# Attention read followed by a soft mixture of experts: the dispatch division behind layer one, wider transfers, a new order

## The chip, the cores and the metric

The kernel runs on one core of a Trainium2 chip. The metric is the time on the device in microseconds (us), the median of three runs. Engines are written as in the profile: PE is the matrix engine, PEld its weight loads, DVE the vector engine, ACT the scalar engine, POOL the third elementwise engine, SP the engine whose queue issues nearly all DMA transfers.

## The reference, cut to what matters

All data are float32. The attention part makes 4,352 rows of 512 numbers; the expert part treats all of them as one batch.

```
# attention: x (8,8,512,64), state (8,8,32,64)
a     = softmax(x state^T / 8);  xread = a state
a2    = softmax(state x^T / 8);  sread = a2 x
rows  = concat(xread, sread)              # 4352 x 512 after regrouping
# soft mixture of experts: 8 experts, 4 slots each
logits = rows phi                         # 4352 x 32
d = exp(logits - max over rows); d /= sum over rows + 1e-9
slot_input = d^T rows                     # 32 x 512
h = relu(slot_input[e] w1[e]); slot_out[e] = h w2[e]
c = softmax(logits over the 32 slots)
out = c slot_out                          # 4352 x 512
```

The sum under d is positive, so relu(v / s) = relu(v) / s: the division may stand before or behind the first layer.

## The kernel before, in words

The 51 MB that move are x (8 batches), the two weight matrices (33.5 MB together) and the output (8.9 MB). Every instruction is placed by hand: `ORDER` is a list of steps such as `x1.7.0`, each name a small function, and every engine runs its own instructions in the order in which they come up there. A `!` behind a step sends its copy to DVE, otherwise to ACT. The lists `HOMES` say which buffer each new tile takes: `b` the eight PSUM banks, `h` eleven half tiles of 128x512, `big` five tiles of 8 KB a partition, `wide` eight of 16 KB a partition.

**The attention stage** (up to about 76 us) walks through the eight batches. For each batch and each half h of its heads: `X`, `xe` transpose and scale x; `S` makes the scores; `q`, `m1`, `sub`, `x1`, `l1`, `rr`, `mul`, `aT` are one softmax (DVE transposes and reduces, POOL subtracts and multiplies, ACT takes the exponential); `m2`, `e2`, `E`, `ee`, `R`, `sr` are the other; `A`, `ae` turn the first one's result back; `Lx` makes the logits of the batch. Batches go in pairs k = 0 to 3 into a running maximum, a running sum `l_row` and a running dispatch product `y`: `mx`, `mk`, `bm`, `nme` give the new maximum, `al` the factor by which what is there shrinks, `dx`, `dT`, `dTe`, `T`, `tt`, `Px` the pair's own product, and `Y` adds it as y = y * factor + part. The state rows do the same in two halves (`Ls`, `Lr`, `msx`, `als`, `dsx`, `D`, `Ps`, `Ys`). The last two additions are `Y.3` and `Ys.1`. Then `Wd`, `We` make the reciprocal `rl` of the sum, `SI` transposes y, and `SIe` multiplies by `rl` and spreads the result into `si_m`, a block-sparse operand zeroed ahead of time (`windows`).

**The first layer** is the steps `W`, 16 of them, eight matmuls each on the page's count, at line 805. `hc`, `ht`, `hr` copy, transpose, sum and rectify one half of the hidden units and spread it into `h_m`, zeroed by `hz` on POOL. **The second layer** is the steps `u.k.hf.e` at line 868, for four column blocks k of the output. Each block ends in `c.k` (copy), `s.k` (a matmul that sums the partial rows, and a copy of its result to `so_r`), `o.k.0` and `o.k.1` (four matmuls each with the combine weights, `os` for the state rows) and eight copies `oc.k.q.j` into the output tile. In between, `cm`, `cx`, `cd`, `cb` make the combine weights. One output transfer goes for each (k, q), two for those in `HALVED`.

**The loads** stand in `loads()`. Seven weight transfers are issued at the start; `ld.0` to `ld.15` are the rest. SP takes its transfers strictly in order, and each waits until its target buffer has been read for the last time: a `big` tile until the batch of x or the weight tile in it is used up, `w_half` until four half tiles are free, `w_an` until the two `an` tiles are.

Of the kernel before, what the change touches and what calls it, by code (L numbers as in the profile page):

```python
# [980 lines left out]
```

## Time and profile before

| what | value |
|---|---|
| median of 3 runs | 129.79 us (129.78 to 129.86) |
| the profiled execution, own time | 130.58 us |
| its span, first to last instruction | 128.8 us |
| PE, DVE, ACT, POOL busy | 115.7, 88.6, 74.1, 44.7 us |
| moved by DMA | 51.76 MB, 402 GB/s over the span |

The profiled execution is 0.79 us above the median, and 1.78 us of it lie outside its span. Busy time of PE counts pipelined matmuls from issue to a modelled end, so 90% busy does not mean PE at its peak. The DMA share is the mean over sixteen DMA engines and passes 1.00 in some stretches.

### The profile page before, as it was taken

Reading aid. Unit: us, or ns where it says so; the run is one execution under the profiler, and the core shown is the slowest. Engines: PE = TensorE matmul, PEld = TensorE weight load, DVE = VectorE, ACT = ScalarE, POOL = GpSimd, SP = SyncE. Lnnn points to the kernel's source line nnn. Section 1 sums busy time; section 2 is a strip of 40 time slices with the busy share of each in tenths; the row PEclk is TensorE's granted clock in tenths of the full one; section 3 lists DMA queues with packets and bytes.
Section 4 is the critical chain, followed back from the end, with each engine's and each line's share of the span. In section 5 each row is a group of like instructions: output and inputs, shape, how many; then the busy total and the mean of one; then the engine's idle time right before and its main releaser. Section 6 shows DMA issues by size and latency. Waiting matters only on the chain.

```text
span 128.8 us, 4863 instructions
## 1 busy us (share of the span) xinstructions
PE 115.7 (90%) x2080; PEld 83.6 (65%) x2080; DVE 88.6 (69%) x206; ACT 74.1 (58%) x178; POOL 44.7 (35%) x62
## 2 busy tenths in 40 slices
PE   6979999999999999999998969999999999998400
PEld 3647768588659769587887759934594667576100
DVE  3069999999999999999998687651073254173700
ACT  3038999999998899999953601030203753151600
POOL 2105175395459363386693205653010000000000
PEclk9999999999999999999999999999999999999955
DMA  4999999999999999999999999999999999999991
GB/s 90 374 401 453 417 438 399 445 417 455 415 407 458 427 412 417 416 421 425 438 445 417 415 408 410 420 425 433 435 443 407 389 396 416 417 384 420 374 416 78
DMA packets 7366, 51.76 MB, mean 402 GB/s; under 512 B 816, under 2 KB 944, under 8 KB 3760
## 3 DMA queue, kind: packets, MB, share of 16 engines
q1 hardware_dynamic: 7200, 51.19, 95.6%
q8 instruction: 16, 0.26, 0.7%
q10 hardware_dynamic: 144, 0.26, 0.6%
q14 instruction: 6, 0.05, 0.1%
HBM read 42.53 MB, written 8.91 MB: 399 GB/s over the span
## 4 chain that ended last, share of the span: by engine, by line
PE 54%; DVE 17%; ACT 16%; issue 5%; POOL 2%; DVEq 1%; POOLq 0%
PE so_ps L868 12%; PE h_ps L805 11%; PE o L897 7%; ACT xt L271 4%; PE spin L292 3%; ACT q L365 3%; DVE nm L437 3%; PE sc L340 3%; DVE q L353 3%; ACT e L442 2%; DVE m L358 2%; ACT eT L268 2%; DVE aT L384 2%; PE an_ps L450 2%; ACT an L268 2%
## 5 line engine op out<-in xcount | busy, mean ns | idle before, releaser
L271 ACT ACTIVATE xt<-xt_ps 128x512 f32<-128x512 f32 x30 | 16.9, 628 | 6.6 <-PE xt_ps L391 4.7
L362 POOL TENSOR_TENSOR q<-q,m 128x512 f32<-128x512 f32 x14 | 14.7, 1049 | 15.7 <-DVE m L358 9.2
L379 POOL TENSOR_TENSOR q<-q,rr 128x512 f32<-128x512 f32 x16 | 16.6, 1049 | 6.6 <-DVE rr L375 2.9
L326 PE MATMUL xt_ps<-ident,x 128*128 128x128 f32 x112 | 15.7, 277 | 0.0
L868 PEld LDWEIGHTS so_ps<-w,h_m 128*32 128x32 f32 x432 | 11.5, 110 | 6.1 <-issue 5.6
L868 PE MATMUL so_ps<-w,h_m 128*32 128x128 f32 x432 | 15.1, 275 | 0.0
L805 PE MATMUL h_ps<-w,si_m 128*32 128x512 f32 x128 | 14.6, 594 | 0.4 <-DVE si_m L776 0.4
L268 ACT COPY out<-o 128x512 f32<-128x512 f32 x18 | 9.5, 596 | 7.4 <-PE o L897 7.4
L326 PEld LDWEIGHTS xt_ps<-ident,x 128*128 128x128 f32 x112 | 12.4, 141 | 1.9 <-DVE q L353 0.8
L268 DVE COPY out<-o 128x512 f32<-128x512 f32 x14 | 9.1, 686 | 4.7 <-PE o L897 4.5
L442 ACT ACTIVATE e<-sc,nm 128x512 f32<-128x512 f32 x16 | 11.5, 724 | 0.0
L805 PEld LDWEIGHTS h_ps<-w,si_m 128*32 128x32 f32 x128 | 8.6, 110 | 4.1 <-issue 3.2
L384 DVE STREAM_TRANSPOSE aT<-q 128x512 f32<-128x512 f32 x16 | 10.9, 687 | 0.1
L365 ACT ACTIVATE q<-q 128x512 f32<-128x512 f32 x16 | 10.2, 655 | 1.1 <-POOL q L362 1.1
L437 DVE TENSOR_REDUCE nm<-sc 128x1 f32<-128x512 f32 x16 | 10.5, 662 | 0.0
L897 PE MATMUL o<-lt_all,so_r 32*128 32x512 f32 x64 | 10.3, 629 | 0.0
L368 DVE TENSOR_REDUCE ls<-q 128x16 f32<-128x512 f32 x16 | 10.2, 666 | 0.0
L353 DVE STREAM_TRANSPOSE q<-sc 128x512 f32<-128x512 f32 x14 | 9.8, 697 | 0.1
L450 PE MATMUL eT_ps<-ident,e 128*128 128x128 f32 x64 | 9.7, 280 | 0.0
L450 PE MATMUL an_ps<-ident,aT 128*128 128x128 f32 x64 | 9.5, 277 | 0.0
L268 ACT COPY eT<-eT_ps 128x512 f32<-128x512 f32 x16 | 9.3, 604 | 0.2
L358 DVE TENSOR_REDUCE m<-q 128x16 f32<-128x512 f32 x14 | 9.2, 661 | 0.1
(144 smaller groups left out, 198.4 us busy)
## 6 DMA issues: line engine op xcount, KB each, us to landing
w<-w_in SPq DMA_DIRECT2D x10, 2048.0 KB, 26.1
w<-w_in SPq DMA_DIRECT2D x9, 1024.0 KB, 13.6
out_x<-out SPq DMA_DIRECT2D x5, 1024.0 KB, 6.8
x<-x_in SPq DMA_DIRECT2D x2, 2048.0 KB, 15.5
out_x<-out SPq DMA_DIRECT2D x6, 512.0 KB, 5.5
x<-x_in SPq DMA_DIRECT2D x2, 1024.0 KB, 14.6
x<-x_in SPq DMA_DIRECT2D x2, 512.0 KB, 6.6
w_half<-w_in SPq DMA_DIRECT2D x4, 256.0 KB, 15.2
```

The source lines that it names most:

```text
L268: (dve.tensor_copy if Z["dve"] else act.copy)(out, in_)
L271: (dve.tensor_scalar_mul if Z["dve"] else act.mul)(out, in_, by)
L326: pe.transpose(p[:, P * j : P * j + P], x_at(b, g, j), ident)
L362: pool.tensor_tensor(v, v, R[b][f"m1{h}"].broadcast_to([P, 16, NS]), op=ALU.subtract)
L365: act.activation(R[b][f"q{h}"], R[b][f"q{h}"], AF.Exp)
L379: pool.tensor_tensor(v, v, R[b]["rr"][:, 16 * h : 16 * h + 16].broadcast_to([P, 16, NS]), op=ALU.mult)
L437: dve.tensor_reduce(out=r[f"nm2{h}"], in_=r[f"sp{h}"], axis=AX.X, op=ALU.max, negate=True)
L442: act.activation(r[f"e2{h}"], r[f"sp{h}"], AF.Exp, bias=r[f"nm2{h}"], accum_out=ls[:, b % 2, 32 + h, 0:1])
L450: pe.transpose(p[:, j, :], r[f"{src}{h}"][:, P * j : P * j + P], ident)
L805: pe.matmul(h_ps[hf][32 * kt : 32 * kt + 32, :], si_m[kt // 2][:, 256 * (kt % 2) + 32 * e : 256 * (kt % 2) + 32 * e + 32], wt[1, hf, e, kt ...
L868: pe.matmul(so[k][32 * i : 32 * i + 32, :], h_m[hf][:, 256 * i + 32 * e : 256 * i + 32 * e + 32], wt[2, c, e, 4 * hf + i][:, col : col + n ...
L897: pe.matmul(o[j], so_r[hf][rows, col : col + 128], lt_all[rows, 4 * q : 4 * q + 4, :].rearrange("p b s -> p (b s)"), start=True, stop=True,)
```

## The change

1. `SIe` becomes two plain copies, one for each tile of `si_m`, with no factor. `We` makes `rl` as before; `hr` now uses it: one instruction rectifies and multiplies all four blocks, one copy spreads them (before: four rectifying instructions that also spread).
2. The last two additions to y change places: `Ys.1` first, with a factor that carries y past both maxima at once (`al.3`), then `Y.3` adds the pair's product times the factor of the state half. `l_row` likewise.
3. The five `big` tiles and the eleven half tiles are slices of one tile each, so that a transfer can fill neighbours: the weight loads go out as 13 transfers behind the first seven instead of 20 in 16 steps, `w_half` as one of 1 MB instead of four, `w_an` as one instead of two, and six of the 1 MB loads as three of 2 MB. Block 1 of the output goes out as one transfer of 2 MB when all its eight copies are done (`WHOLE`), instead of two of 1 MB.
4. `ORDER` is new, and with it `HOMES`. The steps are the same but for `SIe` and `ld`.

```diff
 ORDER = """
...
-Y.1 Ve.1! Lr.1 ld.5 Lu.2 al.3 msx.1 als.1 Px.2 Ys.0 dsx.1 D.1 T.3 Ps.1 tt.3 Lu.3 Y.2 ld.6 ld.7 Px.3 Lus.1 Wd Y.3
-Ys.1 SI We SIe W.0.0 cm.0 W.0.1 W.0.2 W.0.5 ld.8 ld.9 ld.10 W.0.6 W.0.7 W.0.3 ld.11 cx.0 W.0.4 hc.0 W.1.0 lkp.1!
...
+nme.2 ee.7.0 srT.4 l1.6.1 rr.6 V.0 ae.5.0 sr.5 ld.2 x1.7.1
+l1.7.1 R.6.0 R.6.1 srT.5 sub.7.0 mul.6.0 ae.5.1 srTe.4 R.7.0 x1.7.0 l1.7.0 ee.7.1 R.7.1 sr.6 dx.2 srTe.5 rr.7 aT.6.0
...
+ld.3 Ls.1 Px.1 A.6.1 nme.3 dx.3 dT.3 Lse.1 Lr.1 tt.2 al.2 keep.3 Y.1 Ps.0 dTe.3 ae.6.1! T.3 Lus.0 msx.1 Ve.1! Ue.1
+dsx.1 Px.2 D.1 Ps.1 Lu.2 Ys.0 ld.4 al.3 Lus.1 lkp.1 als.1 tt.3 ld.5 ld.6 Px.3 Y.2 Ys.1 Y.3 Lu.3 Wd SI SIe.0! SIe.1!
+W.0.0 W.0.1 W.0.2 We W.0.5 W.0.6 W.0.7 cm.1 W.0.3 W.0.4 cx.1 ld.7 W.1.0 hc.0 ht.0 cd.1 W.1.1 W.1.2 ld.8 hz hr.0
...
+cb.2 u.0.1.4 u.0.1.5 u.0.1.6 u.0.1.7 c.0 u.1.0.6 u.1.0.7 ld.9 u.1.1.0 s.0! o.0.0 oc.0.0.0! u.1.1.1 o.0.1 oc.0.1.0
+oc.0.1.1 ld.10 ld.11 oc.0.1.2 ld.12 oc.0.1.3 oc.0.0.1! oc.0.0.2 u.1.1.2 oc.0.0.3! u.1.1.3 u.1.1.4 u.1.1.5 u.1.1.6
+u.1.1.7 u.2.0.0 u.2.0.1 c.1! s.1 os.0 o.1.0 oc.1.0.0! oc.1.0.1 oc.1.0.2! u.2.0.2 u.2.0.3 o.1.1 u.3.0.0 u.3.0.1
...
+oc.1.1.0! oc.1.1.1! oc.1.0.3 al.0 oc.1.1.2 oc.1.1.3 u.3.0.4 u.3.0.5 c.2 s.2! o.2.0 oc.2.0.0! oc.2.0.1! oc.2.0.2
+oc.2.0.3 u.3.0.6 o.2.1! oc.2.1.0 oc.2.1.1! oc.2.1.2 u.3.0.7 u.3.1.0 u.3.1.1 u.3.1.2 u.3.1.3 u.3.1.4 u.3.1.5 u.3.1.6
...
+WHOLE = (1,)
...
-    yield from [("big", [t]) for t in early[:3]]
+    yield "big", early[:1]
+    yield "bigs", early[1:3]
     yield from pairs[6:]
-    yield from [("big", [t]) for t in early[3:]]
+    yield "bigs", early[3:]
     yield "half", [second[0][5]]
     yield "an", [second[0][6]]
-    yield from [("big", [t]) for t in (second[0][7], *second[1][:3])]
+    yield "big", second[0][7:]
+    yield "bigs", second[1][:2]
+    yield "big", second[1][2:3]
...
+    bigs = big.tile([P, NHOMES["big"], 2 * F], F32, name="bigs")
+    def big_tile():
+        return bigs[:, int(next(turn["big"]))]
+    def big_pair():
+        i, j = sorted(int(next(turn["big"])) for _ in range(2))
+        assert j == i + 1
+        return bigs[:, i : j + 1].rearrange("p i f -> p (i f)")
...
         def al(k):
-            rescale(X2[k])
+            r = X2[k]
+            if k == 3:
+                i = r["i"]
+                act.activation(
+                    al_all[:, r["c"]], nm_all[:, i - 1 : i], AF.Exp, bias=nm_all[:, Q[1]["c"]], scale=-1.0
+                )
+            else:
+                rescale(r)
...
         def Lu(k):
+            if k == 3:
+                pool.tensor_tensor(r["lx"], r["lx"], al_all[:, Q[1]["c"]], op=ALU.mult)
+                pool.tensor_tensor(l_row, l_row, r["lx"], op=ALU.add)
...
         def Y(k):
+            if k == 3:
+                dve.scalar_tensor_tensor(
+                    out=y, in0=part, scalar=al_all[:, Q[1]["c"]], in1=y, op0=ALU.mult, op1=ALU.add
+                )
+            else:
+                add_y(r, part)
...
         def Ys(k):
-            add_y(Q[k], Q[k]["psp"])
+            add_y(X2[3] if k else Q[k], Q[k]["psp"])
...
-        def SIe():
-            for k in range(4):
-                dve.tensor_tensor(
-                    slots(si_m[k // 2], k % 2),
-                    Z["p"][:, k, :].rearrange("p (e c) -> p e c", c=4),
-                    Z["rl"].rearrange("p (e c) -> p e c", c=4),
-                    op=ALU.mult,
-                )
+        def SIe(i):
+            copy(slots(si_m[i]), Z["p"][:, 2 * i : 2 * i + 2, :].rearrange("p k (e c) -> p k e c", c=4))
...
-            for ft in range(4):
-                dve.tensor_scalar_max(slots(h_m[hf], ft), t[:, ft, :].rearrange("p (e c) -> p e c", c=4), 0.0)
+            rl = Z["rl"].rearrange("p (o n) -> p o n", o=1).broadcast_to([P, 4, NS])
+            dve.scalar_tensor_tensor(out=t, in0=t, scalar=0.0, in1=rl, op0=ALU.max, op1=ALU.mult)
+            dve.tensor_copy(slots(h_m[hf]), t.rearrange("p f (e c) -> p f e c", c=4))
...
+            if k in WHOLE:
+                if (q, j) == (1, 3):
+                    nc.sync.dma_start(out_x[k], out_t[k].rearrange("p q j s -> p (q j s)"))
```

## Rows read from the trace of the kernel before

**Rows 1.** Stretches A:B: us, busy time of each engine, PE clock, DMA share, GB/s.
```profile
core 0: us, PE busy (x) PEld busy (x) DVE busy (x) ACT busy (x) POOL busy (x), PEclk, DMA share, GB/s
10.00:20.00 10.00, 10.00 (x165) 7.09 (x162) 9.97 (x23) 9.73 (x23) 4.96 (x7) 1.00 1.03 439
30.00:40.00 10.00, 9.83 (x183) 7.27 (x176) 9.83 (x22) 9.62 (x25) 5.70 (x7) 1.00 1.00 424
60.00:67.40 7.40, 7.24 (x159) 6.50 (x158) 7.18 (x20) 6.31 (x20) 6.01 (x8) 1.00 1.02 432
67.40:76.30 8.90, 7.43 (x154) 5.60 (x146) 6.67 (x22) 3.33 (x11) 2.03 (x11) 1.00 1.00 420
76.30:97.00 20.70, 20.70 (x328) 14.73 (x328) 10.48 (x32) 2.82 (x6) 7.22 (x7) 1.00 1.03 425
97.00:120.80 23.80, 23.22 (x411) 14.60 (x403) 10.39 (x20) 10.43 (x23) 0.00 (x0) 1.00 0.97 400
102.40:103.40 1.00, 0.93 (x19) 0.57 (x9) 0.89 (x2) 0.76 (x3) 0.00 (x0) 1.00 0.56 234
114.00:115.00 1.00, 1.00 (x33) 0.84 (x36) 1.00 (x2) 0.97 (x2) 0.00 (x0) 1.00 0.71 295
119.20:121.00 1.80, 1.52 (x12) 0.53 (x6) 1.80 (x4) 1.57 (x4) 0.00 (x0) 1.00 0.80 324
```

**Rows 2.** Weight transfers of line 207, time from issue to landing.
```profile
DMA to landing us min/median/max: 9.8/17.1/37.9
```

**Rows 3.** Timeline, SP's output transfers: start, length, operation.
```profile
102.65 1.78 SPq L912 DMA_DIRECT2D out_x<-out  x3
104.89 0.86 SPq L928 DMA_DIRECT2D out_s<-out_s  x1
106.61 9.02 SPq L912 DMA_DIRECT2D out_x<-out  x4
120.04 2.77 SPq L912 DMA_DIRECT2D out_x<-out  x4
```

**Rows 4.** Timeline, from the last additions to the first layer.
```profile
74.69 0.35 DVE L577 SCALAR_TENSOR_TENSOR y<-y,al_all,px_ps 128x128 f32<-128x128 f32 x1 [0.35 <-PE px_ps L656]
75.07 0.35 DVE L577 SCALAR_TENSOR_TENSOR y<-y,al_all,ps_ps 128x128 f32<-128x128 f32 x1
75.55 0.35 DVE L749 RECIPROCAL rl<-rl 128x32 f32<-128x32 f32 x1
75.57 0.30 PE L758 MATMUL si_ps<-ident,y 128*128 128x128 f32 x1 [0.62 <-DVE rl L748]
76.04 0.49 DVE L776 TENSOR_TENSOR si_m<-si_ps,rl 128x32 f32<-128x32 f32 x4
76.29 0.91 PE L805 MATMUL h_ps<-w,si_m 128*32 128x512 f32 x4 [0.42 <-DVE si_m L776]
```

**Rows 5.** Timeline, the softmax of the last batch on ACT, DVE and POOL.
```profile
61.39 0.63 ACT L365 ACTIVATE q<-q 128x512 f32<-128x512 f32 x1
62.06 0.61 ACT L268 COPY an<-an_ps 128x512 f32<-128x512 f32 x1
62.53 0.62 ACT L268 COPY eT<-eT_ps 128x512 f32<-128x512 f32 x1
62.52 1.27 DVE L368 TENSOR_REDUCE ls<-q 128x16 f32<-128x512 f32 x2
63.55 3.09 POOL L379 TENSOR_TENSOR q<-q,rr 128x512 f32<-128x512 f32 x3
65.32 2.07 DVE L384 STREAM_TRANSPOSE aT<-q 128x512 f32<-128x512 f32 x3
```

**Rows 6.** Timeline, weight loads of PE in the second layer.
```profile
97.56 0.16 PEld L868 LDWEIGHTS so_ps<-w,h_m 128*32 128x32 f32 x8
97.98 0.31 PEld L897 LDWEIGHTS o<-lt_all,so_r 32*128 32x128 f32 x8 [0.27 <-ACT so_r L268]
106.16 0.31 PEld L897 LDWEIGHTS o<-lt_all,so_r 32*128 32x128 f32 x8 [0.20 <-ACT out L268]
```

More of the change, by code (lines that the diff above doesn't have):

```diff
@@ new lines @@
+E.1.0 x1.1.0 X.3.3 e2.1.1 xe.3.3 X.3.0 xe.3.0 X.3.2 X.3.1 E.1.1 e2.2.1 aT.0.0 ee.1.0 m1.2.1 E.2.1 l1.1.0 srT.0 q.2.0
+m2.2.0 sub.1.1 X.4.1 R.1.0 xe.3.1 mul.0.1 xe.3.2 S.3 m1.2.0 x1.1.1 l1.1.1 rr.1 srTe.0 e2.2.0 E.2.0 sub.2.1 x1.2.1
+A.0.0 ee.1.1 R.1.1 m2.3.0 ee.2.0 e2.3.0 aT.0.1 sub.2.0 ae.0.0 x1.2.0 mul.1.0 R.2.0 aT.1.0 ld.0 sr.1 ee.2.1 mul.1.1
+q.3.0 aT.1.1 xe.4.1 Lx.0.0 Lx.0.1 m1.3.0 Lx.1.0 srT.1 srTe.1 A.1.0 A.0.1 ae.0.1 X.4.3 X.4.0 m2.3.1 xe.4.3 e2.3.1
+l1.2.1 l1.2.0 rr.2 Lx.1.1 keep.0 R.2.1 xe.4.0 X.4.2 xe.4.2 E.3.1 mx.0 mk.0 sr.2 q.3.1 m1.3.1 sub.3.0 X.5.3 sub.3.1
@@ new lines @@
+mx.1 xe.6.0 E.5.1 x1.5.0 l1.5.0 xe.6.3 sub.5.1 x1.5.1 S.6 mul.4.1 sr.4 l1.5.1 Px.0 mul.4.0 e2.5.0 Y.0 E.5.0 keep.1
+rr.5 mul.5.1 Lse.0 X.7.1 ee.5.1 pv.1 mk.1 bm.1 X.7.3 mul.5.0 m2.6.0 ae.3.1 aT.4.0 ee.5.0 Lr.0 xe.7.1 R.5.0 R.5.1
+e2.6.0 m2.6.1 A.2.1 nme.1 msx.0 lkp.0! aT.4.1 q.6.0 X.7.2 dx.1 dT.1 xe.7.3 aT.5.0 ae.2.1 xe.7.2 m1.6.0 X.7.0 xe.7.0
+q.6.1 m1.6.1 A.4.0 dTe.1 E.6.0 ee.6.0 S.7 m2.7.0 als.0 aT.5.1 T.1 sub.6.1 dsx.0 Lx.4.0 Lx.4.1 sub.6.0 Lx.5.0 Lx.5.1
+e2.6.1 m2.7.1 e2.7.0 pv.2! ae.4.0 q.7.1 m1.7.1 A.4.1 x1.6.1 E.7.0 x1.6.0 E.6.1 mx.2 ae.4.1 q.7.0 e2.7.1 A.5.1 A.5.0
@@ L69 @@
+oc.2.1.3! u.3.1.7 c.3! s.3! os.1 o.3.0! oc.3.0.0! oc.3.0.1 oc.3.0.2! oc.3.0.3 o.3.1 oc.3.1.0! oc.3.1.1 oc.3.1.2!
+spin.3 oc.3.1.3
 """
@@ L137, in home @@
     def home(pool, kind, n, name):
-        i = next(turn[kind], None)
-        if i is None:
-            return pool.tile([P, n], F32, tag=kind, name=name, bufs=NHOMES[kind])
+        i = next(turn[kind])
         return pool.tile([P, n], F32, tag=kind + i, name=name, bufs=1)
-    def big_tile(name):
-        return home(big, "big", 2 * F, name)
+    bigs = big.tile([P, NHOMES["big"], 2 * F], F32, name="bigs")
[5 more added lines that the diff above has]
+        return bigs[:, i : j + 1].rearrange("p i f -> p (i f)")
     def wide_tile(name):
         return home(wide, "wide", 4 * F, name)
-    xs_a = big_tile("x0_a")
-    xs_b = big_tile("x0_b")
+    xs_a = big_tile()
+    xs_b = big_tile()
     stT_sb = xs_b[:, F:].rearrange("p (q g a b n) -> p q g a b n", q=4, g=2, a=2, b=2)
@@ L271, in scale @@
             (dve.tensor_scalar_mul if Z["dve"] else act.mul)(out, in_, by)
+        work = wk.tile([P, NH, S], F32, name="work")
+        an_all = wk.tile([P, AN, F], F32, name="an_all")
+        an_turn = itertools.count()
         def half(name):
-            return home(wk, "h", S, name)
+            return work[:, int(next(turn["h"]))]
         def bank(shape, name):
@@ L316, in load @@
             if kind == "half":
-                tiles = [half(f"w_half{i}") for i in range(4)]
+                at_h = sorted(int(next(turn["h"])) for _ in range(4))
+                assert at_h[3] == at_h[0] + 3
+                tiles = [work[:, at_h[0] : at_h[3] + 1].rearrange("p i s -> p (i s)")]
             elif kind == "an":
-                tiles = [wk.tile([P, F], F32, tag="an", name=f"w_an{i}", bufs=AN) for i in range(2)]
+                tiles = [an_all.rearrange("p i f -> p (i f)")]
             load_w(tiles)
@@ L465, in ae @@
             if "an" not in r:
-                r["an"] = wk.tile([P, NJ, 4, 2, NS], F32, tag="an", name=f"an{b}", bufs=AN)
+                r["an"] = an_all[:, next(an_turn) % AN].rearrange("p (j g h n) -> p j g h n", j=NJ, g=4, h=2)
             copy(r["an"][:, :, :, h, :], r[f"anp{h}"].rearrange("p j (g n) -> p j g n", g=4))
@@ L664, in Y @@
         def Y(k):
-            add_y(X2[k], X2[k]["pxp"].rearrange("p h d -> p (h d)"))
+            r = X2[k]
+            part = r["pxp"].rearrange("p h d -> p (h d)")
+            if k == 3:
+                dve.scalar_tensor_tensor(
+                    out=y, in0=part, scalar=al_all[:, Q[1]["c"]], in1=y, op0=ALU.mult, op1=ALU.add
+                )
+            else:
+                add_y(r, part)
         def Ls(k):
@@ L793, in h_zero @@
         def h_zero():
-            t = big_tile("h_m")
+            t = big_tile()
             pool.memset(t, 0.0)
@@ L909, in out_copy @@
             n = 2 if (k, q) in HALVED else 4
-            if j % n == n - 1:
-                part = slice(512 * (j + 1 - n), 512 * (j + 1))
-                nc.sync.dma_start(out_x[k, q][:, part], out_t[k][:, q, j + 1 - n : j + 1].rearrange("p i s -> p (i s)"))
+            if k in WHOLE:
+                if (q, j) == (1, 3):
+                    nc.sync.dma_start(out_x[k], out_t[k].rearrange("p q j s -> p (q j s)"))
+            elif j % n == n - 1:
+                c = 2048 * q + 512 * j + 512
+                nc.sync.dma_start(
+                    out_x[k][:, c - 512 * n : c], out_t[k][:, q, j + 1 - n : j + 1].rearrange("p i s -> p (i s)")
+                )
         def out_st(c):
@@ L977 @@
     r = _run(nc, [arrays], core_ids=[0]).results[0]
-    ox = r["out_x"].reshape(4, 2, P, 2, 2, 4, P).transpose(1, 5, 3, 4, 6, 0, 2).reshape(B, S, 512)
+    ox = r["out_x"].reshape(4, P, 2, 2, 2, 4, P).transpose(2, 5, 3, 4, 6, 0, 1).reshape(B, S, 512)
     os_ = r["out_s"].reshape(2, P, 2, B, NS).transpose(3, 4, 0, 2, 1).reshape(B, NS, 512)
```

78 lines of the change are left out of this document (31 added, 47 removed), and 8 rows, old and new, of the table b.

## The prediction, made before the changed kernel ran

> **What bounds the kernel now.** I read the stretches first. Up to 67 us DVE is busy 97 to 100% of the time, with ACT hardly behind; from 67.4 to 76.3 DVE, ACT and POOL loosen, and PE, at 7.43 of 8.90 us, works through a chain of short steps; from 76.3 to 120.8 PE is busy 20.70 of 20.70 and 23.22 of 23.80 us, always at the full clock [rows 1]. So the compute side is one chain: a DVE-bound attention stage, a chain of hand-overs to the first layer, and a PE stream of 44 us whose start sets its end. The second bound runs beside it: the DMA share is about 1.00 from the first loads to the last output. It drops in three places, all after the loads run out: 0.56 over 1.0 us at 102.4, 0.71 over 1.0 us at 114, 0.80 over 1.8 us at 119.2 [rows 1]. These are 0.44 + 0.29 + 0.36 = 1.09 us of empty queue, each filled when the next output is issued (k=0 from 102.65, k=2 among the four that SP issues from 106.61 to 115.63, k=3 from 120.04) [rows 1, 3]. So an output is late each time, because PE and the copies are late: if PE's stream moves earlier by t, the end does too, until about 1.1 us are used up; behind that the DMA queue alone sets the end. If PE's stream gets later, the end gets later by as much.
>
> **The change, part by part.** *Last additions and division.* Today Y.3 runs at 74.69, Ys.1 at 75.07, SI at 75.57, the first SIe at 76.04, the first layer at 76.29, after two of the four SIe instructions [rows 4]. With Ys.1 first, only Y.3 stands behind the last product: 75.07 - 74.69 = 0.38 us saved, if Ys.1's operand is there before (Ps.1 and the state half's maximum come ahead of Px.3 in the new order too). SI's matmul ends at 75.57 + 0.30 = 75.87, the reciprocal at 75.90 and SIe starts at 76.04 [rows 4]: the division itself holds SIe back by only some 0.09 us, since it runs beside the transpose. The first of two copies then replaces two instructions of 0.49 / 4 = 0.12 us; a copy of twice their size takes between 0.12 and 0.25 us, I take 0.17: 0.08 us saved. If PE has to wait for both copies, this is 0.10 us lost instead. Sum 0.38 + 0.09 + 0.08 = 0.55 us, between 0.37 and 0.60. The two instructions that `hr` gets for its four, and `We`, cost nothing on the path: PE has the steps W.1.1 and W.1.2 between `ht.0` and the first use of `h_m`, whose first four matmuls alone take 0.91 us [rows 4]; without that cover a few tenths would be lost, twice.
>
> *Tail of the attention stage.* ae.6.0, ae.7.1 and keep.3 go from DVE to ACT, ae.6.1 and keep.2 come to DVE, and Ps.0 goes behind dT.3 on PE. By adding up the steps in DVE's new order behind the last maximum, tt.3 and Y.3 come 0 to 0.4 us earlier; ACT gets a copy of some 0.5 us ahead of dx.3, which takes back part. I take 0.2 us saved.
>
> *The attention stage's new order.* Step for step DVE has the same work ahead of the last aT.7.1, to 0.1 us. ACT does not: ahead of x1.7.0, the last exponential of the last batch, come four more copies `ae` (starts of two neighbours are 62.53 - 62.06 = 0.47 us apart [rows 5]) and two small instructions, while Ve.0 and two small ones go behind it. That is 4 * 0.47 + 0.35 - 0.85 = 1.4 us later. Today it ends at 62.02, and the sums l1 that use it start at 62.52 with two in a row; then rr, three POOL multiplications back to back to 66.64, and aT.7.1 to 67.39 [rows 5]. In the new order only one of the two sums waits for x1.7.0: from 63.42 the sum (0.63), sr and rr (0.7), two multiplications (3.09 / 3 = 1.03 each) and one transpose (2.07 / 3 = 0.69) give 67.5, that is 0.1 us later. Idle time of DVE is 0.03 us in the stretch 10 to 20, 0.17 in 30 to 40 and 0.22 in 60 to 67.4 [rows 1]; a new order can win or lose such amounts in each stretch. I take 0.1 us lost, between 0.5 won and 1.0 lost.
>
> *The PE stream.* Today a step u runs between s.0 and o.0.0, and PE still waits 0.27 us for so_r [rows 6]. The new order has none there, and none between s.2 and o.2.0: PE waits longer by one step u each, whose eight weight loads take 0.16 to 0.24 us; 2 * 0.22 = 0.44 us lost. In front of o.1.1 PE waits 0.20 us for a bank [rows 6]; u.3 now starts behind o.1.1, which leaves a bank more: 0.20 us won. Net 0.24 us lost, between 0 and 0.5.
>
> *Loads.* The bytes are the same. Joined transfers wait for the later of two buffers, but the shortest time from issue to landing is 9.8 us [rows 2], so a load that is issued some us later still lands in its turn: nothing. As to the rate, the stretch with the small transfers, 76.3 to 97, moves 425 GB/s at a share of 1.03, that with 2 MB transfers, 30 to 40, 424 at 1.00 [rows 1]: 413 against 424 for a full queue, at most 2.6% of 20.7 us = 0.5 us. It brings the loads' end forward, but the next output isn't there then, so by itself it only widens the hole at 102.4. I count 0, and 0.5 as the far end. The Trainium skill (DMA: Bandwidth & Descriptors, section Anatomy of one DMA) gives each transfer a fixed cost of about 2.0 us beside its bytes; eight transfers fewer would by that be up to 16 us. The trace disagrees for a full queue: in 20.7 us with a dozen transfers the rate stays at 425 GB/s [rows 1], so that cost is covered by the transfers around it.
>
> *Block 1 in one transfer.* Its first half is issued at 106.61 today; the other half behind it [rows 3]. As one it waits for the last copy. Ahead of it the queue holds block 0 and the state block, 2.36 MB, which at 400 GB/s [rows 1] last 5.9 us from about 103.4, to 109.3. With o.1.1 two steps u and a wait earlier, the last copy ends near 108, and data start about 0.75 us behind an issue (102.65 to 103.4 [rows 1, 3]): 108.8. So nothing, and up to 0.5 us if the copies end 1 us later. The dips behind it could still take that up.
>
> **Sum.** -0.55 - 0.2 + 0.1 + 0.24 = -0.41 us, well inside the 1.1 us that the queue can give. The profiled execution took 130.58 us with a span of 128.8; taken off both, the span becomes 128.4. Against the median of 129.79 it is **129.4 us**.
>
> **The rivals.** *A: the attention stage gets shorter.* DVE and ACT are both near full, and the idle rows above are all that an order can win, some 0.5 us; with 0.55 + 0.2 + 0.5 - 0.24 = 1.0 us PE would be at the point where the full queue takes over: 128.4 to 129.0. For it speaks that DVE's work ahead of the last maximum is smaller by a copy and `keep.3`; against it, that the wait before bm.3 is PE's, whose order there is the same.
>
> *B: the last batch's softmax comes late, slower.* The place is x1.7.0 on ACT. By 1.4 us late it costs 0.1; each further us goes straight through rr.7, POOL, aT.7.1 and Lx.7.1 to the first layer. It decides from some 2.1 us late on, since 0.67 us more eat the 0.41 of the forecast and the 0.26 that a measurement can tell. ACT has only 0.27 us idle in 10 to 20 [rows 1], so its list hardly hides a late step. Priced at 0.7 to 1.6 us beyond the sum: 130.1 to 131.
>
> *C: nothing measurable.* The 0.55 us at the hand-over are won, but o.0.0 and o.2.0 wait the full 0.5 us together, and the 2 MB transfer leaves a hole of 0.5 us that the dips do not hide: 129.55 to 130.05. For it speaks that the queue, not PE, ends the kernel.
>
> *D: transfers have a price of their own in the full queue,* of the size that the two stretches leave room for: 413 against 424 GB/s, 0.5 us, and PE comes early enough to use it: 128.6 to 129.0. It needs A's early PE as well. The Trainium skill's fixed cost per transfer, at the same place, is the rule that speaks for it.
>
> **How the numbers follow.** The forecast (129.0 to 129.55) gets 0.35, A 0.11, D 0.06, B 0.25, C 0.23. A run-to-run difference of 0.2%, 0.26 us, is about what a measurement can tell, so faster is below 129.53 and slower above 130.05: faster 0.52, same 0.23, slower 0.25. The range 128.5 to 130.6 leaves out some of A and the upper part of B, 0.15 together; the likeliest case's own is 129.0 to 129.55.
>
> **What would show it.** Right: one addition between the last product and SI, the first layer at about 75.6 (from 76.29), the last output issue at about 0.4 us earlier than 120.04 for the first of four, the hole at 119 smaller. Wrong steps would be seen as: ACT or POOL as the one waited for ahead of aT.7.1; waits of over 0.6 us ahead of o.0.0 and o.2.0; a share far under 1 near 109; a rate over 425 GB/s in 76 to 97. The forecast falls if the first layer starts later than 76.3, or if the new order makes SP issue a load so late that the queue empties before 102.

## The result: slower by 0.75%, and the profile after

The changed kernel takes 131.06 us (median of 13 runs) where the kernel before has 129.86 in the 13 runs beside it: ratio 1.0075, 95% interval 1.0046 to 1.0104. The ratios here leave out the few runs in which the chip was in a slower state (one of these 26, at 133.14 us), so they differ a little from the quotient of two medians. Forecast were 129.4 us and faster; 131.06 also lies above the range of 128.5 to 130.6. The profiled execution has 131.25 us and a span of 129.4 (before: 130.58 and 128.8).

The stretches of the kernel after; the columns are those of [rows 1].

```profile
core 0: us, PE busy (x) PEld busy (x) DVE busy (x) ACT busy (x) POOL busy (x), PEclk, DMA share, GB/s
97.00:121.50 24.50, 23.17 (x411) 14.58 (x402) 11.11 (x21) 9.60 (x21) 0.00 (x0) 1.00 0.94 388
101.00:123.00 22.00, 19.55 (x370) 13.09 (x369) 9.90 (x19) 9.95 (x21) 0.00 (x0) 1.00 0.93 384
102.00:104.00 2.00, 2.00 (x50) 1.50 (x40) 0.29 (x1) 1.59 (x4) 0.00 (x0) 1.00 0.64 264
114.00:115.00 1.00, 1.00 (x12) 0.24 (x7) 0.82 (x2) 0.73 (x2) 0.00 (x0) 1.00 0.50 213
120.00:122.00 2.00, 1.44 (x12) 0.44 (x5) 2.00 (x4) 1.86 (x4) 0.00 (x0) 1.00 0.70 283
76.30:97.00 20.70, 20.59 (x329) 11.77 (x333) 11.39 (x28) 2.29 (x5) 7.22 (x7) 1.00 1.01 427
```

The kernel before over 101 to 123 us, for comparison:

```profile
101.00:123.00 22.00, 19.22 (x369) 12.90 (x361) 10.34 (x19) 9.74 (x21) 0.00 (x0) 0.99 0.97 397
```

While weights are loaded the rate has not changed: 427 GB/s against 425 in the same stretch [rows 1]. The loss shows behind the loads. The three holes in the outputs' queue have become wider: the share is 0.64 over two us at 102 (before 0.56 over one), 0.50 at 114 (0.71), 0.70 over two at 120 (0.80 over 1.8). Over 101 to 123 the share is 0.93, in the kernel before 0.97: 0.04 of 22 us, 0.9 us more of empty queue.

SP's output transfers of the kernel after, in its timeline:

```profile
102.86 2.86 SPq L946 DMA_DIRECT2D out_x<-out  x3
105.89 1.05 SPq L964 DMA_DIRECT2D out_s<-work  x1
108.50 0.33 SPq L943 DMA_DIRECT2D out_x<-out  x1
114.52 2.74 SPq L946 DMA_DIRECT2D out_x<-out  x2
119.77 0.33 SPq L964 DMA_DIRECT2D out_s<-work  x1
120.75 2.77 SPq L946 DMA_DIRECT2D out_x<-out  x4
```

The last group goes out at 120.75, 0.71 us later than before [rows 3]. So the outputs are late because PE and the copies are. Where they become late is read backwards. The hand-over from the last product (PE, 74.47) over the additions Y.2, Ys.1 and Y.3 (DVE, 74.34, 74.78 and 75.25) to the first layer (PE, 76.36), in the timeline of the kernel after:

```profile
74.34 0.30 DVE L595 SCALAR_TENSOR_TENSOR y<-y,al_all,px_ps 128x128 f32<-128x128 f32 x1
74.78 0.35 DVE L595 SCALAR_TENSOR_TENSOR y<-y,al_all,ps_ps 128x128 f32<-128x128 f32 x1
75.25 0.35 DVE L699 SCALAR_TENSOR_TENSOR y<-px_ps,al_all,y 128x128 f32<-128x128 f32 x1
76.03 0.36 DVE L280 COPY work<-si_ps 128x64 f32<-128x64 f32 x2 [0.42 <-PE si_ps L796]
...
74.47 0.45 PE L687 MATMUL px_ps<-st,tt 64*32 64x64 f32 x16
...
75.66 0.33 PE L796 MATMUL si_ps<-ident,y 128*128 128x128 f32 x1 [0.41 <-DVE y L699]
76.36 1.14 PE L835 MATMUL h_ps<-bigs,work 128*32 128x512 f32 x8 [0.36 <-issue]
```

From the start of Y.3 to the first layer it is 76.36 - 75.25 = 1.11 us; before it was 76.29 - 74.69 = 1.60 [rows 4]: 0.49 us less. But half of this is paid just ahead of Y.3. Y.2, the addition in front, and the last product in the kernel before:

```profile
74.03 0.31 DVE L577 SCALAR_TENSOR_TENSOR y<-y,al_all,px_ps 128x128 f32<-128x128 f32 x1
...
74.16 0.45 PE L656 MATMUL px_ps<-st,tt 64*32 64x64 f32 x16
```

From Y.2 to Y.3 it was 74.69 - 74.03 = 0.66 us, and Y.3 waited for the product. Now it is 75.25 - 74.34 = 0.91 us: Ys.1 stands between them and runs until 75.13, when the product is there since 74.92. From Y.2 to the first layer it is 2.02 us instead of 2.26, so the hand-over wins 0.24 us, not 0.49.

Y.2 itself starts 0.31 us later, 74.34 instead of 74.03. That is less than what the attention stage loses, because PE has a pause in the trace of the kernel before, in the middle of the product Px.1. The two rows of that product there, then its one row in b3_whole, a kernel of the experiments with the same order of steps:

```profile
69.39 0.44 PE L656 MATMUL px_ps<-st,tt 64*32 64x64 f32 x14
70.15 0.29 PE L656 MATMUL px_ps<-st,tt 64*32 64x64 f32 x2 [0.32 <-issue]
```

```profile
69.24 0.44 PE L657 MATMUL px_ps<-st,tt 64*32 64x64 f32 x16
```

PE waits there for nothing that the profile shows, and all that follows is some 0.5 us late: counted from DVE's first transpose, the first layer starts at 67.91 us in this trace and at 67.40 in that of b3_whole. In how many of the timed executions PE pauses like this is not known.

From the first layer to PE's last matmul it takes 45.08 us (76.36 to 121.44) where it took 44.44 (76.29 to 120.73).

What the attention stage loses, it loses near 60 us. DVE, PE and POOL of the kernel after, in its timeline:

```profile
59.11 1.05 POOL L380 TENSOR_TENSOR work<-work,m 128x512 f32<-128x512 f32 x1 [1.16 <-DVE m L376]
...
59.81 1.29 DVE L283 TENSOR_SCALAR mk<-mask,mx 128x4 f32<-128x4 f32 x1
...
60.09 1.01 DVE L376 TENSOR_REDUCE m<-work 128x16 f32<-128x512 f32 x1
60.09 0.98 POOL L808 MEMSET work<- 128x512 f32 x2
...
61.25 0.36 PE L558 MATMUL bm_ps<-mk,rep 128*128 128x5 f32 x2 [0.65 <-DVE m L376]
...
61.64 0.16 DVE L603 TENSOR_REDUCE nm_all<-bm_ps 128x1 f32<-128x5 f32 x1 [0.28 <-PE bm_ps L558]
...
62.43 0.22 DVE L392 TENSOR_REDUCE rr<-ls 128x34 f32<-128x68 f32 x1
```

The new order gives the tiny multiplication `mk.2` (four columns) to DVE, where the kernel before had it on ACT. It lasts 1.29 us there and ends at 61.10, together with POOL's two fills of `windows` (61.07), which the new order puts here as well. The reduction behind it ends at 61.10 too, bm and nm_all follow late, and rr.6 starts at 62.43.

The second loss is in PE's weight loads of the second layer, in the timeline of the kernel after:

```profile
98.20 0.31 PEld L928 LDWEIGHTS o<-lt_all,work 32*128 32x128 f32 x8 [0.58 <-DVE work L280]
...
100.10 0.29 PEld L928 LDWEIGHTS o<-lt_all,work 32*128 32x128 f32 x2 [0.17 <-DVE out L280]
...
105.98 0.31 PEld L928 LDWEIGHTS o<-lt_all,work 32*128 32x128 f32 x8 [0.20 <-issue]
...
112.01 0.31 PEld L928 LDWEIGHTS o<-lt_all,work 32*128 32x128 f32 x8 [0.57 <-DVE work L280]
...
113.92 0.29 PEld L928 LDWEIGHTS o<-lt_all,work 32*128 32x128 f32 x2 [0.17 <-DVE out L280]
```

The load of o.2.0 in the kernel before:

```profile
111.31 0.31 PEld L897 LDWEIGHTS o<-lt_all,so_r 32*128 32x128 f32 x8 [0.30 <-DVE so_r L268]
```

o.0.0 waits 0.58 us for the copy behind s.0 (0.27 before [rows 6]), o.2.0 waits 0.57 (0.30 before). Inside o.0.1 and o.2.1 there are two new waits of 0.17 for a bank. Ahead of o.1.1, at 105.98, the idle 0.20 us of [rows 6] are still there, now with no bank named as what ended them.

### The profile page after: what moved, and what is told of

The parts are those of the page before. It is cut to its first block, busy times and chain, and to the rows that moved or that the text cites. A ratio compares the mean times of both kernels' runs of the same rounds, so it can differ in the third digit from the quotient of the medians.

```text
span 129.4 us, 4835 instructions
## 1 busy us (share of the span) xinstructions
PE 115.7 (89%) x2080; PEld 80.0 (62%) x2080; DVE 89.7 (69%) x201; ACT 73.2 (57%) x177; POOL 44.7 (35%) x62
## 4 chain that ended last, share of the span: by engine, by line
PE 55%; DVE 25%; ACT 9%; issue 3%; POOL 1%; DVEq 0%; ACTq 0%
PE so_ps L899 10%; PE o L928 6%; PE h_ps L835 6%; PE sr_ps L493 4%; ACT work L460 3%; PE spin L308 3%; PE an_ps L468 3%; ACT work L283 3%; DVE work L402 3%; DVE nm L455 3%; PE eT_ps L468 3%; DVE m L376 2%; PE t_ps L653 2%; PE sc L358 2%; DVE work L371 2%
## 5 line engine op out<-in xcount | busy, mean ns | idle before, releaser
L283 ACT ACTIVATE work<-xt_ps 128x512 f32<-128x512 f32 x30 | 17.2, 626 | 6.8 <-PE xt_ps L409 4.4
L380 POOL TENSOR_TENSOR work<-work,m 128x512 f32<-128x512 f32 x14 | 14.6, 1048 | 18.5 <-DVE m L376 16.0
L397 POOL TENSOR_TENSOR work<-work,rr 128x512 f32<-128x512 f32 x16 | 16.5, 1049 | 3.0 <-DVE rr L393 2.0
L460 ACT ACTIVATE work<-sc,nm 128x512 f32<-128x512 f32 x16 | 11.5, 724 | 0.2 <-DVE nm L455 0.2
L928 PE MATMUL o<-lt_all,work 32*128 32x512 f32 x64 | 10.5, 630 | 0.8 <-DVE work L280 0.8
L899 PE MATMUL so_ps<-w,bigs 128*32 128x128 f32 x304 | 11.0, 274 | 0.0
L402 DVE STREAM_TRANSPOSE work<-work 128x512 f32<-128x512 f32 x16 | 10.8, 685 | 0.1
L383 ACT ACTIVATE work<-work 128x512 f32<-128x512 f32 x16 | 10.5, 665 | 0.1
L386 DVE TENSOR_REDUCE ls<-work 128x16 f32<-128x512 f32 x16 | 10.5, 672 | 0.0
L835 PE MATMUL h_ps<-w,work 128*32 128x512 f32 x88 | 10.4, 593 | 0.0
## 6 DMA issues: line engine op xcount, KB each, us to landing
bigs<-w_in SPq DMA_DIRECT2D x3, 1024.0 KB, 11.8
```

The costliest lines, as they stand in the source:

```text
L283: (dve.tensor_scalar_mul if Z["dve"] else act.mul)(out, in_, by)
L380: pool.tensor_tensor(v, v, R[b][f"m1{h}"].broadcast_to([P, 16, NS]), op=ALU.subtract)
L397: pool.tensor_tensor(v, v, R[b]["rr"][:, 16 * h : 16 * h + 16].broadcast_to([P, 16, NS]), op=ALU.mult)
L402: dve.transpose(r[f"aT{h}"], r[f"q{h}"])
L460: act.activation(r[f"e2{h}"], r[f"sp{h}"], AF.Exp, bias=r[f"nm2{h}"], accum_out=ls[:, b % 2, 32 + h, 0:1])
L835: pe.matmul(h_ps[hf][32 * kt : 32 * kt + 32, :], si_m[kt // 2][:, 256 * (kt % 2) + 32 * e : 256 * (kt % 2) + 32 * e + 32], wt[1, hf, e, kt ...
```

## The experiments

Starts differ between the profiles: DVE's first transpose (the expectations call it VectorE's first instruction) begins anywhere from 7.76 to 8.84 us, and everything behind it moves along. So stages are compared as distances: "to rr.6" and "to layer 1" count from DVE's first transpose, "PE stream" from the first layer to PE's last matmul. "Share" is the DMA share of 101 to 123 us. Ratios are to the kernel before, timed beside each batch. There is one trace of each kernel, and kernels with the same steps up to a mark differ there by up to 0.5 us (before and b3_whole at layer 1, by the pause above), so a difference of 0.2 or 0.3 us in a cell counts only where a wait of its own is read beside it.

| kernel | to rr.6 | to layer 1 | PE stream | share | ratio (95%) |
|---|---|---|---|---|---|
| before | 53.27 | 67.91 | 44.44 | 0.97 | |
| after | 54.04 | 67.97 | 45.08 | 0.93 | 1.0075 (1.0046 to 1.0104) |
| b1_hand | 53.29 | 67.22 | 44.41 | 0.99 | 0.9988 (0.9969 to 1.0007) |
| b2_loads | 53.42 | 67.94 | 44.45 | 0.96 | 1.0008 (0.9985 to 1.0031) |
| b3_whole | 53.29 | 67.40 | 44.45 | 0.98 | 1.0008 (0.9983 to 1.0032) |
| h1_attn_before | 53.29 | 67.56 | 45.14 | 0.97 | 1.0019 (1.0000 to 1.0038) |
| a7_win | 53.60 | 67.50 | 45.09 | 0.97 | 1.0066 (1.0033 to 1.0100) |
| a2_mk | 53.43 | 67.36 | 45.08 | 0.94 | 1.0025 (0.9991 to 1.0058) |
| a1_tt2 | 53.96 | 67.69 | 45.08 | 0.92 | 1.0048 (1.0019 to 1.0076) |
| a3_cover | 54.26 | 68.18 | 44.72 | 0.93 | 1.0043 (1.0012 to 1.0073) |
| a5_three | 53.44 | 67.17 | 44.72 | 0.98 | 1.0012 (0.9989 to 1.0035) |
| b4_cover | 53.30 | 67.33 | 44.47 | 0.98 | 1.0002 (0.9973 to 1.0031) |
| h2_b | | | | | 0.9997 (0.9964 to 1.0030) |
| h4_b | 53.44 | 67.19 | 44.38 | 0.99 | 0.9969 (0.9940 to 0.9998) |

The first four take the change apart. **b1_hand**: the kernel before with the new hand-over alone (items 1 and 2 of the change; here the order of the last steps).

```diff
-tt.3 Lu.3 Y.2 ld.6 ld.7 Px.3 Lus.1 Wd Y.3 Ys.1 SI We SIe W.0.0 cm.0 W.0.1 W.0.2
+tt.3 Y.2 ld.6 ld.7 Px.3 Lus.1 Lu.3 Wd Ys.1 Y.3 SI SIe.0! SIe.1! W.0.0 W.0.1 W.0.2 We cm.0
```

> The kernel before, with the hand-over alone: no division in front of the first layer, two copies for the sparse operand, the last two additions as in the changed kernel. Theory 1 (compute chain): the changed kernel's own trace has 1.11 us from the start of the last Y addition that follows the product to the first layer's first matmul, where before had 1.60, so the first layer starts at 75.8 (76.29 before) and the end comes 0.4 to 0.5 us earlier, about 129.4 against 129.86. Theory 2 (the transfers set the end, an earlier PE finds a full queue): the first layer starts earlier but the time stays within 0.2 us of before.

The first layer comes 0.69 us earlier than in the kernel before, but some 0.5 of that is the pause in that trace: against b3_whole it is 0.18 us, less than theory 1's 0.4 to 0.5 and near the 0.24 read above. The time falls by 0.12%, 0.16 us, and its interval reaches past no change. The stretch:

```profile
101.00:123.00 22.00, 17.88 (x323) 11.55 (x313) 10.34 (x19) 8.40 (x18) 0.00 (x0) 1.00 0.99 409
```

The share is 0.99 (0.97 before, 0.98 in b3_whole): next to no hole is left in the queue. Whether the full queue or the small win of the chain keeps the time from falling further, these numbers do not tell apart.

**b2_loads** (the kernel before with the joined loads) and **b3_whole** (with block 1 as one transfer):

```diff
-    yield from [("big", [t]) for t in early[:3]]
+    yield "big", early[:1]
+    yield "bigs", early[1:3]
```

```diff
+WHOLE = (1,)
```

> The kernel before, with the wider loads alone: one tile for the big tiles and one for the half tiles, 13 weight transfers behind the first seven instead of 20. Theory 1: loads have 9.8 us or more between issue and landing, so nothing moves: 129.9, within 0.2 us of before; the DMA rate between 76 and 97 us goes up by at most 2%. Theory 2 (joined transfers wait for the later of two buffers, and slices of one tile may bring waits of their own): 130.4 to 130.9, and PE or SP waits on loads appear.

> The kernel before, with block 1 of the output in one transfer of 2 MB alone. It is issued where the second half is today, 108.7. Theory 1: the queue still holds block 0 until about 109.3, so a hole of at most 0.3 us opens near 109 and PE, not the queue, sets the end: 129.9 to 130.1. Theory 2: a hole of 0.5 to 1 us near 109 that nothing behind it makes up for: 130.4 to 130.9.

Both are at 1.0008, with intervals up to 1.0032: neither form of the transfers makes the 0.75%. In b2_loads the first layer comes late, at 67.94, and there is a pause of POOL ahead of the third multiplication of the last softmax. The only other kernel with joined tiles and the old attention order, h1_attn_before, has the same; b2_loads first:

```profile
65.06 2.06 POOL L394 TENSOR_TENSOR work<-work,rr 128x512 f32<-128x512 f32 x2 [0.33 <-issue]
```

```profile
64.51 2.05 POOL L395 TENSOR_TENSOR work<-work,rr 128x512 f32<-128x512 f32 x2 [0.33 <-issue]
```

None of the four traces with separate tiles and this order has it, nor has the changed kernel's. What makes it is open.

**h1_attn_before**: the changed kernel with the attention's order of the kernel before.

```diff
-sub.7.1 mk.2! bm.2 ee.6.1 E.7.1 m1.7.0 l1.6.0 windows nme.2 ee.7.0 srT.4 l1.6.1 rr.6
...
+l1.6.0 A.5.0 ee.7.0 sub.7.0 A.4.0 mx.2 mk.2 bm.2 l1.6.1 rr.6
...
+al.1 al.2 windows Lu.1
...
```

> The changed kernel with the attention stage in the order of before (with the new hand-over), everything from the first layer on as changed. Theory 1: half of the loss is the attention stage's order (aT.7.1 of the last batch 0.67 us later, the last product's transpose 0.3 us later), half the PE stream behind it (0.6 us longer), so this gives first layer at 75.8 and 129.9 to 130.3. Theory 2 (transfers): as slow as the changed kernel, 130.9 to 131.1. Theory 3 (the attention order is harmless, all is lost behind the first layer): 130.9 as well, but with the first layer at 75.8 and PE's stream longer by over 1 us.

rr.6 is back at 53.29 and the ratio at 1.0019, while the PE stream keeps its 45.14 us. With the old order of the attention most of the loss in time is gone. That alone does not make it the greater part: h2_b, below, takes back the other half of the order and loses as little.

The next four undo one suspected cost each in the changed kernel. **a7_win** moves the fills, **a2_mk** moves the multiplication:

```diff
-m1.7.0 l1.6.0 windows nme.2
+m1.7.0 l1.6.0 nme.2
...
-Lu.0 al.1 Lu.1
+Lu.0 al.1 windows Lu.1
```

```diff
-sub.7.1 mk.2! bm.2
+sub.7.1 mk.2 bm.2
```

> The changed kernel with one step moved: GpSimd's two fills with zeros (step windows) go behind step al.1, where the kernel before had them; the multiplication mk.2 stays on VectorE. Theory M (the fills hold VectorE up: 1.29 us for mk.2 while they run, 0.13 for its like elsewhere): mk.2 lasts under 0.3 us, rr.6 starts 0.5 to 0.9 us earlier than 62.43, the last transpose of the attention ends 0.3 to 0.6 us earlier than 68.05, and the time is 130.4 to 130.8 where the changed kernel has 131.06. Rival N (mk.2 itself is slow on VectorE, by its operands): mk.2 still lasts about 1.3 us and the time stays at 131.0 to 131.1.

> The changed kernel with step mk.2 on ScalarE, as in the kernel before; the fills stay where the change put them. Theory M: VectorE is held up by the fills all the same (its next reduction ends when they end, about 61.1), and on ScalarE mk.2 stands behind two copies that end at 60.86, so the row maximum comes no earlier: gain 0 to 0.2 us, time 130.9 to 131.1. Rival N (the slow thing is this multiplication on VectorE): the reduction behind it ends at 60.6 instead of 61.10, gain 0.3 to 0.5 us, time 130.5 to 130.8.

DVE and POOL of a7_win in its timeline, then ACT, DVE and POOL of a2_mk:

```profile
59.22 0.37 DVE L283 TENSOR_SCALAR mk<-mask,mx 128x4 f32<-128x4 f32 x1
59.50 0.67 DVE L376 TENSOR_REDUCE m<-work 128x16 f32<-128x512 f32 x1
...
58.52 1.05 POOL L380 TENSOR_TENSOR work<-work,m 128x512 f32<-128x512 f32 x1 [1.17 <-DVE m L376]
```

```profile
60.08 0.31 ACT L283 ACTIVATE mk<-mask,mx 128x4 f32<-128x4 f32 x1
...
60.23 0.69 DVE L376 TENSOR_REDUCE m<-work 128x16 f32<-128x512 f32 x1
...
60.40 0.99 POOL L808 MEMSET work<- 128x512 f32 x2
```

Without the fills `mk.2` still lasts 0.37 us and ends at 59.59, when POOL's subtraction ends (58.52 + 1.05 = 59.57). Beside the fills, the reduction in a2_mk takes its usual 0.69 us. So neither theory was whole: in these traces it is the multiplication that is held up and not the reduction, and POOL's subtraction holds it up as its fills do, for as long as POOL goes on without a pause. My expectation for a2_mk also had ACT wrong: it runs `mk.2` ahead of its two copies, at 60.08. rr.6 comes 0.61 us earlier there, 0.44 in a7_win. Up to `mk.2` all DVE instructions of a2_mk and of the changed kernel start within 0.1 us of each other, counted from the first transpose, so the 0.61 us are the work of this one step. In time a2_mk points to the gain (1.0025); a7_win does not (1.0066), although its profiled execution does. The two intervals overlap, so the times do not settle it; the traces do.

The Trainium skill (SBUF — State Buffer, section Who interferes with whom) says that VectorE and GpSimd share one pair of SBUF ports, that a `tensor_scalar` that uses both of VectorE's ports excludes any GpSimd instruction, that the one which comes second waits for the whole of the other, and that a `tensor_reduce` never contends on trn2. The three traces agree: 1.29 us behind a subtraction and two fills, 0.37 behind the end of one subtraction, and reductions at 0.69 beside fills. Whether `mk.2` used both ports, no trace shows. Weighed against the diff beforehand, this would have made `mk.2!` a suspect.

**a1_tt2** and **a3_cover**:

```diff
-            r["tt"] = sm.tile([P, 2, 2, NS], F32, tag="tt", name=f"tt_{k}", bufs=1)
+            r["tt"] = sm.tile([P, 2, 2, NS], F32, tag="dx" if k == 3 else "tt", name=f"tt_{k}", bufs=1)
```

```diff
-u.1.1.0 s.0! o.0.0
+s.0! u.1.1.0 o.0.0
...
-c.2 s.2! o.2.0 oc.2.0.0! oc.2.0.1! oc.2.0.2 oc.2.0.3 u.3.0.6 o.2.1! oc.2.1.0 oc.2.1.1! oc.2.1.2 u.3.0.7
+c.2 s.2! u.3.0.6 o.2.0 oc.2.0.0! oc.2.0.1! oc.2.0.2 oc.2.0.3 u.3.0.7 o.2.1! oc.2.1.0 oc.2.1.1! oc.2.1.2
```

> The changed kernel with the tile tt of the last batch in another buffer, so that step tt.3 need not wait for the last product of step Px.2 (74.02 against 73.57 for its own input). Theory T (this wait is on the path from the attention to the first layer): the last addition and the first layer come 0.2 to 0.45 us earlier, time 130.6 to 130.9. Rival (another wait ends last, the sums of the last batch or Px.3's left operand): first layer at 76.36 as before, time 131.0 to 131.1.

> The changed kernel with one step u of TensorE put between s.0 and o.0.0, and one between s.2 and o.2.0 and one more ahead of o.2.1: TensorE has a product to work on while VectorE copies the transposed values. Theory C (these copies are exposed: TensorE's weight load waits 0.58 and 0.57 us, 0.27 and 0.30 in the kernel before): both waits under 0.35, TensorE's last matmul 0.3 to 0.6 us earlier after the first layer (45.08 us from first layer to end becomes 44.5 to 44.8), time 130.6 to 130.85 if the outputs' queue gives half of it back or less. Rival Q (the transfers set the end): TensorE ends earlier and the time stays at 130.95 to 131.1.

The transpose tt.3, first in the kernel after, then in a1_tt2:

```profile
74.10 0.32 DVE L664 STREAM_TRANSPOSE tt<-t_ps 128x128 f32<-128x128 f32 x1 [0.21 <-PE px_ps L687]
```

```profile
74.17 0.31 DVE L664 STREAM_TRANSPOSE tt<-t_ps 128x128 f32<-128x128 f32 x1
```

The new order puts T.3 ahead of Px.2, which still reads the only tile `tt`; with a second buffer the wait of 0.21 us goes, and the first layer comes 0.28 us earlier (0.08 of it arise ahead of rr.6). In a3_cover the wait ahead of o.0.0 falls to 0.29 us, that ahead of o.2.0 to 0.30:

```profile
98.49 0.31 PEld L928 LDWEIGHTS o<-lt_all,work 32*128 32x128 f32 x8 [0.29 <-DVE work L280]
...
112.30 0.31 PEld L928 LDWEIGHTS o<-lt_all,work 32*128 32x128 f32 x8 [0.30 <-DVE work L280]
```

and the PE stream to 44.72 us, 0.36 less. The times fall by 0.3%, with intervals that overlap that of the changed kernel: in time neither gain is shown.

**a5_three**, all three repairs (`mk.2` on ACT):

> The changed kernel with the three edits together: mk.2 on ScalarE, tt.3 in another buffer, steps u as cover for the copies behind s.0 and s.2. Theory C (the three costs add up, 0.6 + 0.3 + 0.35 us): the first layer starts 66.9 to 67.3 us after VectorE's first instruction (67.97 in the changed kernel, 67.91 before), TensorE's stream from there lasts 44.6 to 44.8 us (45.08, 44.44 before), time 129.9 to 130.2, the level of the kernel before or 0.2 under it, since part of it goes to the outputs' queue. Rival Q (the order's loss lies in the transfers): time stays at 130.7 or more.

As in theory C: first layer 0.80 us earlier, PE stream 0.36 shorter, 1.16 together. The ratio goes from 1.0075 to 1.0012, some 0.8 us. The three single repairs add to 1.1% and together give 0.6%; with intervals of 0.3% to either side on each, that need not be a difference.

**b4_cover** (b1_hand with one more cover behind s.0 and s.2) and **h4_b** ask whether more can be had; **h2_b** (the changed kernel with the order of the kernel before from W.0.0 on; h4_b is the same with the edits of a2_mk and a1_tt2) asks what the second layer's order costs in time.

```diff
-s.0 u.1.1.0 o.0.0! u.1.1.1
+s.0 u.1.1.0 u.1.1.1 o.0.0!
...
-s.2! u.3.0.4 o.2.0
+s.2! u.3.0.4 u.3.0.5 o.2.0
```

```diff
-u.1.1.0 s.0! o.0.0
+s.0 u.1.1.0 o.0.0!
...
-u.3.0.4 u.3.0.5 c.2 s.2! o.2.0
+c.2 u.3.0.2 u.3.0.3 s.2! u.3.0.4 o.2.0
```

> The kernel before with the new hand-over, as in b1_hand, and with one more step u between s.0 and o.0.0 and between s.2 and o.2.0. Theory C: the waits of 0.27 and 0.30 us behind the two copies go, TensorE's stream lasts 43.9 to 44.2 us instead of 44.41. If TensorE set the end, the time would be 129.4 to 129.6; if the outputs' queue does from here on (b1_hand's had no hole left between 102 and 124 us), it stays at 129.7 to 129.9, as b1_hand.

> The changed kernel with the order of the kernel before from the first layer on; its attention, its hand-over, its wide loads and its whole output of block 1 stay. Theory C: the first layer 67.8 to 68.1 us after VectorE's first instruction, as in the changed kernel (67.97), TensorE's stream from there 44.4 to 44.5 us, 0.6 us shorter than in the changed kernel (45.08), so that the holes in the outputs' queue are about those of the kernel before: ratio to it 1.001 to 1.004. Rival (the second layer's order costs nothing, all the loss is in the attention): 1.006 to 1.009, as the changed kernel.

> As h2_b, with mk.2 on ScalarE and tt.3 in another buffer. Theory C: the first layer 66.9 to 67.3 us after VectorE's first instruction, TensorE's stream 44.4 to 44.5 us, no hole over 0.15 us left in the queue from 102 us on except one near 113. The transfers are the floor: ratio 0.996 to 1.000, as b1_hand, although TensorE ends 0.7 us earlier than in the kernel before. Rival (TensorE sets the end): 0.993 to 0.995.

b4_cover misses: the wait ahead of o.0.0 falls only to 0.20 us, the idle time that o.1.1 has too, and the PE stream stays at 44.47, because behind it the loads of o.0.1 now wait for banks:

```profile
97.45 0.31 PEld L910 LDWEIGHTS o<-lt_all,so_r 32*128 32x128 f32 x8 [0.20 <-ACT so_r L268]
...
99.25 0.29 PEld L910 LDWEIGHTS o<-lt_all,so_r 32*128 32x128 f32 x2 [0.63 <-ACT out L268]
```

h2_b lands at 0.9997, below its expected 1.001 to 1.004 but with an interval that reaches them (its profiled execution, at 134.28 us, is 4 us above its median, so its trace is not compared). It rejects the rival: the second layer's order costs time too. With either half of the order taken back, h1_attn_before or h2_b, the time is within 0.4% of the kernel before, and the intervals overlap; so how the lost time divides between the two halves is read from the traces alone. h4_b has the first layer at 67.19, a PE stream of 44.38 us and the stretch

```profile
101.00:123.00 22.00, 18.16 (x333) 11.84 (x325) 10.34 (x19) 8.69 (x19) 0.00 (x0) 0.97 0.99 407
```

Its 129.64 us against 130.22 are a ratio of 0.9969 (0.9940 to 0.9998): the fastest version here, 0.3% under the kernel before and about 1% under the changed one, at the share of b1_hand. Two earlier builds, h2_attn_after (132.81 us) and h4_best (132.35; h4_b with the covers of b4_cover), gave one load step four buffers too many in the list `h`, so that all later tiles moved; their times say nothing on these questions.

## Why the prediction was wrong, step by step

In what follows the distances of the changed kernel are set against b3_whole where the pause of PE in the trace of the kernel before would blur them.

**Hand-over, 0.55 us won: half of it, 0.24.** The division and the addition behind the last product did go: 0.49 us less from Y.3 on. But "only Y.3 stands behind the last product" left out that Ys.1 now stands ahead of Y.3 and is still running when the product comes: 0.25 us. The copies that replace `SIe` saved nothing: PE starts 76.36 - 76.03 = 0.33 us behind the first of them, where it was 76.29 - 76.04 = 0.25.

**The attention's new order, 0.1 us lost: the step that failed.** "Step for step DVE has the same work ahead of the last aT.7.1, to 0.1 us" counted `mk.2` as a small step of the usual length. It took 1.29 us beside POOL, and rr.6 came 0.77 us later (54.04 against 53.27; the six kernels with the old order lie between 53.27 and 53.42). a2_mk, a5_three and h4_b bring it back to 53.43 and 53.44. The place on which rival B was built, x1.7.0 on ACT, did not decide: what came late was DVE's, before it. The term's range, up to 1.0 us lost, holds this, but by another mechanism.

**Tail of the attention, 0.2 us won: nothing.** From rr.6 to tt.3 it is 11.67 us in the changed kernel and 11.6 to 11.8 in the three traces of the old order without a pause of PE or POOL (b1_hand, b3_whole, b4_cover). The wait of tt.3 for its only buffer, 0.21 us, was not seen; a1_tt2 takes it away.

**PE stream, 0.24 us lost: the mechanism right in part, the size wrong, 0.64.** The two uncovered copies cost 0.31 + 0.27 us of waiting more (0.44 forecast). The 0.20 us ahead of o.1.1 are not won: they stay though no bank is named any more, and 0.20 is the least that the waits behind the copies fell to as well (b4_cover). Two bank waits of 0.17 were not forecast. These idle times together exceed the 0.64; what made up for the rest is not read here.

**Loads and block 1 in one transfer, 0: right for the transfers** (b2_loads, b3_whole, to 0.3%), and the share at 109 is no hole in the kernel after. The POOL pause of 0.33 us that goes with joined tiles in the old order was not foreseen; the changed kernel does not have it.

**The queue gives back up to 1.1 us: too much.** These holes were read in an execution that took 130.58 us, 0.79 above the median, with the 0.5 us pause of PE in it. In b3_whole's, without the pause, the share of 0.98 leaves 0.4 us. So the forecast of 129.4, which starts from the median and wants 0.41 us, had just about that room. In the other direction the rule held: PE later by t widens the holes.

In sum the chain is 67.97 + 45.08 - 67.91 - 44.44 = 0.70 us longer than in the trace of the kernel before and 67.97 + 45.08 - 67.40 - 44.45 = 1.20 us longer than in b3_whole's; the time is 1.0 us longer (0.6 to 1.35 by the interval). Against b3_whole, rr.6 comes 0.75 us later, the steps from there to tt.3 take 0.08 more, those from tt.3 to the first layer 0.26 less, and the stream 0.63 more. Which part of a median the starts of each execution make was not measured.

## What to carry to other kernels

A step moved from one engine to another is not priced by its size: ask what the neighbours do at that moment. Here a multiplication by a scalar on DVE stood still beside POOL, and on ACT it did not. A win measured from a mark is a win only if the mark itself has not moved: follow the chain back until both kernels agree. Holes and distances are to be read in an execution at the median, and a second trace of the same order shows which pauses belong to the kernel: here one pause of 0.5 us looked like room in the queue and hid 0.5 us of the loss. A new order needs its one-buffer tiles and its covers looked up step by step: the buffer of one transposed tile and two missing products cost more than the better hand-over won.

## What the runs showed of the hardware that was not expected

In the kernel after, one DVE multiplication of 128x1 beside POOL's subtractions, to be held against the 1.29 us of the 128x4 above:

```profile
57.46 0.13 DVE L283 TENSOR_SCALAR mk<-nm_all 128x1 f32<-128x1 f32 x1
...
55.89 2.05 POOL L380 TENSOR_TENSOR work<-work,m 128x512 f32<-128x512 f32 x2 [4.07 <-DVE m L376]
```

The 128x4 did not get in between POOL's instructions: the subtraction ended at 60.16, the fills began at 60.09, and DVE stood until 61.10. The 128x1 was not held up; why, no run here shows. And the profiles of these kernels start their work up to 1.1 us apart, and some have a pause of 0.3 to 0.5 us on PE or POOL that waits for nothing shown, so that a single profile can differ from the median by nearly as much as the change does.
